# Elementwise work taken off GpSimd, and the first layer's gates run on two DFF chunks at a time

## The chip, the cores and the metric

One NeuronCore of a Trainium2 chip runs the whole kernel. The number that counts is the device time of one launch in microseconds, as a median over runs. Engines are called by the names of the profile: PE (TensorE), DVE (VectorE), ACT (ScalarE), POOL (GpSimd) and SP (SyncE, which issues most DMAs).

## The reference, cut to what matters

Windowed attention (4 batches, 8 heads, 768 positions, head size 64) gives 3072 rows of 512 features. They go through a dense layer with a gate, and then to one of eight experts each.

```python
attn = softmax(q @ k.T / 8 + alibi_bias, local window of 96 and 8 global keys) @ v
x = attn.transpose(0, 2, 1, 3).reshape(3072, 512)
h = x @ w_in                      # w_in: 512 x 2048, float64
g = h - tanh(h)
y = g @ w_out                     # w_out: 2048 x 512, float64
e = argmax(y @ w_gate)            # 8 experts
out = softmax_max * sigmoid(y @ w_output_gate)[e] * (relu(y @ w1[e]) @ w2[e])
```

## The kernel before

**Products in parts.** Each float32 operand of a large product is split into a high part (float32r) and the low rest; a product is three matmuls: high by high, low by high, high by low.

**First layer.** The 3072 tokens are taken in 12 blocks of 256, the 2048 columns of DFF in 16 chunks of 128 (`u`). `moe_h` makes one chunk's h in PSUM: 12 matmuls of 256 columns into half of a bank of the tag `h`, which has two banks. Then come three steps. `gate` makes h squared, tanh h and a polynomial (ACT three instructions, DVE three). `gate2` makes a mask and the product, and takes h - tanh h where the mask says so. `parts` splits the result into `gh` (ACT) and `gl` (POOL). `moe_y` adds the chunk to y: six matmuls of 512 columns, three for each half of the block's tokens.

**Weights of the first layer.** w_in and w_out come as float64 in 32 pieces of 128x512. `m1_split` turns the 64 bits of a number into a float32 with shifts, and then into two parts. Pieces with an even number are decoded by one ACT and three DVE instructions, DVE makes the high part and POOL the low one. Pieces with an odd number take two ACT instructions, one on POOL and two on DVE, ACT makes the high part and POOL the low one.

**Order.** `at(gt, rank, fn)` puts work on an agenda of half units: chunk `u` of block `blk` has its `moe_h` at half unit 32 blk + 2u, its `gate`, `gate2` and `parts` one, two and three half units later, and its `moe_y` four later (five in the last block). Block 0's attention begins at half unit -26. The pieces of the weights are decoded from half unit -31 to 21, so during block 0's attention and its first layer. Later blocks' attention (`plan_att`) lies among the chunks of the block before. `plan_route` sends a finished block's rows to their experts (`rt_evac`, `rt_T`, `rt_logits`, then a scatter that POOL issues). A scheduler that simulates a time line turns the agenda into the order of each engine's instructions. After the last block come eight experts, whose weights are loaded and split meanwhile (`ex_load`, `ex_split`); a first job of 256 rows (`ex_s1`, `ex_s2` of job 0) lies beside the last block's routing.

The lines that matter below: L254 to L273 decode the weights, L491 to L512 are the softmax, L580 is `moe_h`, L595 to L620 are the three steps of the gate, L637 is `moe_y`.

Of the kernel before, what the change touches and what calls it, by code (L numbers as in the profile page):

```python
# [9 lines left out]
F32 = mybir.dt.float32  # L10
# [8 lines left out]
# (h - tanh(h)) / h^3 as a cubic in u = h*h for u <= G_T2, in the form  # L19
# G_C3 * (u + G_C) * ((u + G_A)^2 + G_B); relative error below 3e-7  # L20
# [12 lines left out]
def kernel(  # L33
# [27 lines left out]
    # rows in the static part, for the experts in the order of their tokens  # L61
# [9 lines left out]
    LATE = 3                      # chunks of the last product of all, taken tile by tile  # L71
    W = DM + 2                    # a routed row: y, its scale, its token
# [106 lines left out]
    def load_next(which):  # L179
        if nxt[which] < len(pair_seq):  # L180
# [10 lines left out]
            else:  # L191
# [5 lines left out]
                # the general attention's result where that ran  # L197
# [8 lines left out]
    # weights of the first layer: four groups of four chunks of DFF  # L206
# [11 lines left out]
    def m1_load(i):  # L218
# [14 lines left out]
    def m1_split(i, gt):  # L233
        """float64 bits to float32 (its 24 leading bits), then to two parts"""
# [48 lines left out]
    # ------------------------------------------------------------ constants  # L283
    def constants_first():
# [4 lines left out]
        # value = float(low word) + 2^32 * float(high word)  # L289
# [6 lines left out]
        # the windowed path needs 1 <= n_local <= 97 and n_global <= 32  # L296
# [8 lines left out]
        # where not so, the windowed path takes each token's own value: n_global = 0, n_local = 1  # L305
# [9 lines left out]
    # minus the distance, and -BIG where not kept; a head's scores are taken over its slope  # L315
# [3 lines left out]
    # for each pair of heads, 1 / (8 slope) of the head of a row of the transposed queries  # L319
# [5 lines left out]
    def masks():  # L325
# [35 lines left out]
        # other tiles: columns 0..31 are keys 0..31, column c >= 32 has rel = p + 128 - c  # L361
        d1 = tmp("d1", "gg", 2)
# [10 lines left out]
        # a block's first tile has the same columns in another order  # L373
# [6 lines left out]
    def constants_late():  # L380
# [3 lines left out]
        # tri[k, m] = 1 where k < m  # L384
# [1003 lines left out]
```

## Time and profile before

| | before |
|---|---|
| runs | 1212.83, 1214.79, 1216.89 us (median 1214.79) |
| span of the profiled execution | 1207.3 us, from its first to its last instruction |
| PE busy | 1135.9 us (94%) |
| DVE busy | 904.5 us (75%) |
| ACT busy | 652.1 us (54%) |
| POOL busy | 321.0 us (27%) |

No time is listed for the profiled execution apart from its span. The median of the runs lies 7.5 us above that span (5.5 to 9.6 us for the three), for what a launch does before the first and after the last instruction. Busy shares are means over the span; the stages differ, so the rows below are taken by stage.

### The profile page before, as it was taken

Reading aid. Unit: us, or ns where it says so; the run is one execution under the profiler, and the core shown is the slowest. Engines: PE = TensorE matmul, PEld = TensorE weight load, DVE = VectorE, ACT = ScalarE, POOL = GpSimd, SP = SyncE. Lnnn points to the kernel's source line nnn. Section 1 sums busy time; section 2 is a strip of 40 time slices with the busy share of each in tenths; the row PEclk is TensorE's granted clock in tenths of the full one; section 3 lists DMA queues with packets and bytes.
Section 4 is the critical chain, followed back from the end, with each engine's and each line's share of the span. In section 5 each row is a group of like instructions: output and inputs, shape, how many; then the busy total and the mean of one; then the engine's idle time right before and its main releaser. Section 6 shows DMA issues by size and latency. Waiting matters only on the chain. (4 is left out here: it accounts for less than half of the span.)

```text
span 1207.3 us, 22194 instructions
## 1 busy us (share of the span) xinstructions
PE 1135.9 (94%) x7374; PEld 955.2 (79%) x7374; DVE 904.5 (75%) x2712; ACT 652.1 (54%) x1729; POOL 321.0 (27%) x377
## 2 busy tenths in 40 slices
PE   4876699999999999999999999999899999999996
PEld 3555578888888888888888888888788787888895
DVE  7999997989898889888898888899654434435410
ACT  4666576666657566657566666656443323324411
POOL 3467663423131222222222212233200101101100
PEclk9997899999999999999999999999999999999998
DMA  6643383111111111111111112012365415326200
GB/s 176 176 144 123 111 231 97 49 30 47 42 48 32 45 32 46 38 49 34 37 34 40 47 26 54 8 53 87 124 215 178 134 66 198 124 78 216 108 22 23
DMA packets 128848, 103.23 MB, mean 86 GB/s; under 512 B 101679, under 2 KB 101679, under 8 KB 128720
## 3 DMA queue, kind: packets, MB, share of 16 engines
q1 hardware_dynamic: 124592, 89.06, 25.3%
q0 software_dynamic: 4128, 12.61, 2.7%
q8 instruction: 61, 1.00, 0.3%
q14 instruction: 67, 0.55, 0.2%
HBM read 90.04 MB, written 21.88 MB: 93 GB/s over the span
## 5 line engine op out<-in xcount | busy, mean ns | idle before, releaser
L620 POOL TENSOR_TENSOR gl<-gg,gh 128x256 fp32r<-128x256 f32 x192 | 163.1, 850 | 432.0 <-ACT gh L619 367.6
L580 PE MATMUL ph<-xhi,wh 128*128 128x256 f32 x768 | 224.3, 293 | 10.1 <-DVE tt L599 10.1
L580 PE MATMUL ph<-xlo,wh 128*128 128x256 f32 x768 | 222.0, 289 | 0.1
L580 PE MATMUL ph<-xhi,wl 128*128 128x256 f32 x768 | 221.6, 289 | 0.0
L637 PE MATMUL y<-wh,gh 128*128 128x512 f32 x384 | 162.8, 424 | 7.0 <-ACT gh L619 7.0
L580 PEld LDWEIGHTS ph<-xhi,wh 128*128 128x128 f32 x768 | 148.1, 193 | 23.4 <-DVE tt L599 13.1
L580 PEld LDWEIGHTS ph<-xlo,wh 128*128 128x128 f32 x768 | 148.3, 193 | 10.6 <-issue 2.2
L637 PE MATMUL y<-wl,gh 128*128 128x512 f32 x384 | 153.5, 400 | 0.0
L580 PEld LDWEIGHTS ph<-xhi,wl 128*128 128x128 f32 x768 | 148.4, 193 | 5.6 <-issue 2.2
L637 PE MATMUL y<-wh,gl 128*128 128x512 f32 x384 | 142.2, 411 | 4.6 <-POOL gl L620 4.6
L619 ACT CAST gh<-gg 128x256 fp32r<-128x256 f32 x192 | 78.1, 407 | 122.7 <-DVE gg L613 101.2
L953 DVE SCALAR_TENSOR_TENSOR h2l<-h2p,h2h 128x448 fp32r<-128x448 f32 (+3 forms) x72 | 39.9, 557 | 102.2 <-ACT h2h L952 102.2
L875 DVE TENSOR_TENSOR el<-ex,eh 128x1024 fp32r<-128x1024 f32 x64 | 77.7, 1223 | 50.0 <-ACT eh L874 49.7
L993 POOL DMA_INDIRECT out_dram<-orow,ix x29 | 30.2, 1041 | 291.4 <-ACT orow L988 284.7
L595 ACT ACTIVATE uu<-ph 128x256 f32<-128x256 f32 x192 | 73.0, 380 | 63.7 <-PE ph L580 58.3
L598 DVE SCALAR_TENSOR_TENSOR vt<-uu,ph 128x256 f32<-128x256 f32 x192 | 79.5, 414 | 32.6 <-ACT tt L596 30.9
L952 ACT ACTIVATE h2h<-h2p 128x448 fp32r<-128x448 f32 (+3 forms) x72 | 35.3, 493 | 123.3 <-PE h2p L948 123.0
L874 ACT CAST eh<-ex 128x1024 fp32r<-128x1024 f32 x64 | 66.5, 1049 | 63.8 <-DMA ex<-in_moe_w_dram 48.8
L499 ACT ACTIVATE pr<-pr,sst 128x256 f32<-128x256 f32 (+1 forms) x192 | 92.6, 485 | 13.2 <-DVE sst L491 13.0
L613 DVE COPY_PREDICATED gg<-ss,tt 128x256 f32<-128x256 int32 x192 | 94.6, 493 | 4.9 <-POOL gg L610 1.9
L597 ACT ACTIVATE ss<-uu,ga 128x256 f32<-128x256 f32 x192 | 97.9, 511 | 0.0
L975 PE MATMUL ob<-eh,h2h 128*128 128x512 f32 x232 | 92.8, 400 | 5.3 <-ACT h2h L952 5.1
(194 smaller groups left out, 2686.6 us busy)
## 6 DMA issues: line engine op xcount, KB each, us to landing
ex<-in_moe_w_dram SPq DMA_DIRECT2D x64, 512.0 KB
vv<-vg SPq DMA_DIRECT2D x92, 96.0 KB
srt<-zrow SPq DMA_DIRECT2D x32, 257.0 KB
m<-in_moe_w_in_dram SPq DMA_DIRECT2D x16, 512.0 KB
m<-in_moe_w_out_dram SPq DMA_DIRECT2D x16, 512.0 KB
xr<-srt SPq DMA_DIRECT2D x25, 257.0 KB
qk<-in_q_dram SPq DMA_DIRECT2D x92, 64.0 KB
qk<-in_k_dram SPq DMA_DIRECT2D x92, 64.0 KB
```

Of the source, the lines that this page charges most:

```text
L499: nc.scalar.activation(pr[j][:, c0:], pr[j][:, c0:], AF.Exp, bias=st[:, j : j + 1], scale=-1.0, accum_out=st[:, 2 + j : 3 + j],)
L580: nc.tensor.matmul(ph[:, 0:TB], lw, xx[blk][:, kc, :], start=(n == 0), stop=(n == 3 * KC - 1))
L595: nc.scalar.activation(uu, hps, AF.Square)
L597: nc.scalar.activation(ss, uu, AF.Square, scale=G_S, bias=ga[:, 0:1])
L598: nc.vector.scalar_tensor_tensor(out=vv, in0=uu, scalar=G_C, in1=hps, op0=ALU.add, op1=ALU.mult)
L613: nc.vector.copy_predicated(gg, ss.bitcast(I32), tt)
L619: nc.scalar.copy(gh, gg)
L620: nc.gpsimd.tensor_tensor(out=gl, in0=gg, in1=gh.bitcast(F32), op=ALU.subtract)
L637: nc.tensor.matmul(yb[blk, j], gx[:, j * P : (j + 1) * P], wx[fg][:, sl], start=(u == 0 and n == 0), stop=(u == NF - 1 and n == 2),)
L874: nc.scalar.copy(hi, st)
L875: nc.vector.tensor_tensor(out=ld[e, t][:, sl], in0=st, in1=hi.bitcast(F32), op=ALU.subtract)
L975: nc.tensor.matmul(ob[n, j][0:m, :], gx[:, j * P : j * P + m], wx, start=(f == 0 and i == 0), stop=(f == NF2 - 1 and i == 2),)
```

## The change

In the decode, every piece now goes the way of the even ones, except that ACT makes the high part and DVE the low one. POOL has no part in it.

`moe_h` fills a whole bank with two chunks, `u` and `u + 1`, and only the second of them starts the gate. Each step of the gate then works on 512 columns. The product of `gate2` is on DVE in all blocks, the mask is a Relu on ACT in all blocks (before, in block 0 alone; DVE made it in the others), and the result stays in the tile `vt`. `parts` makes `gl` on DVE. `moe_y` stands two half units later (at 6, and at 7 in the last block), and so does the routing. The tiles change tags: `uu`, `tt` and `gl` share four of 512 columns, `ss` has one, `gh` two. POOL keeps its indirect DMAs, constants and the token numbers of the rows.

```diff
     def m1_split(i, gt):
...
-        by_pool = i % 2 == 1
         def decode():
-            if by_pool:
-                nc.gpsimd.tensor_tensor(out=tw, in0=tw, in1=st[:, :, 1], op=ALU.add)
-                nc.vector.tensor_scalar(out=w_0, in0=w_0, scalar1=29, scalar2=None, op0=ALU.logical_shift_right)
-                nc.vector.scalar_tensor_tensor(
-                    out=ti, in0=ti, scalar=3, in1=w_0, op0=ALU.logical_shift_left, op1=ALU.bitwise_or
-                )
-                return
             nc.vector.tensor_scalar(out=ti, in0=ti, scalar1=3, scalar2=None, op0=ALU.logical_shift_left)
...
         def parts():
-            if i % 2:
-                nc.scalar.copy(hi, tw)
-            else:
-                nc.vector.tensor_copy(hi, tw)
-            nc.gpsimd.tensor_tensor(out=lo, in0=tw, in1=hi.bitcast(F32), op=ALU.subtract)
+            nc.scalar.copy(hi, tw)
+            nc.vector.tensor_tensor(out=lo, in0=tw, in1=hi.bitcast(F32), op=ALU.subtract)
-        nc.scalar.activation(tw, st[:, :, 1], AF.Relu if by_pool else AF.Copy, scale=2.0**-112)
-        if by_pool:
-            nc.scalar.activation(st[:, :, 1], st[:, :, 1], AF.Relu, scale=-(2.0**-80))
+        nc.scalar.activation(tw, st[:, :, 1], AF.Copy, scale=2.0**-112)
...
     def moe_h(blk, u, gt):
-        ph = bank("h", 2, f"ph{blk}_{u}")
+        if u % 2 == 0:
+            ph_t[blk] = bank("h", 2, f"ph{blk}_{u}")
+        ph = ph_t[blk]
+        o_h = (u % 2) * TB
...
-                nc.tensor.matmul(ph[:, 0:TB], lw, xx[blk][:, kc, :], start=(n == 0), stop=(n == 3 * KC - 1))
+                nc.tensor.matmul(
+                    ph[:, o_h : o_h + TB], lw, xx[blk][:, kc, :], start=(n == 0), stop=(n == 3 * KC - 1)
+                )
+        if u % 2 == 0:
+            return
         def tmp(tag, bufs, dt=F32):
-            t = p1.tile([P, TB], dt, tag=tag, bufs=bufs, name=f"{tag}{blk}_{u}")
+            t = p1.tile([P, 2 * TB], dt, tag=tag, bufs=bufs, name=f"{tag}{blk}_{u}")
...
         def gate2():
-            gg = L["gg"] = tmp("gg", 2)
-            if blk < 1:
-                nc.scalar.activation(ss, uu, AF.Relu, bias=nt2[:, 0:1])
-            else:
-                nc.vector.tensor_scalar(out=ss, in0=uu, scalar1=G_T2, scalar2=None, op0=ALU.is_gt)
-            if blk < 2:
-                nc.gpsimd.tensor_tensor(out=gg, in0=vv, in1=uu, op=ALU.mult)
-            else:
-                nc.vector.tensor_tensor(out=gg, in0=vv, in1=uu, op=ALU.mult)
-            nc.vector.copy_predicated(gg, ss.bitcast(I32), tt)
+            nc.vector.tensor_tensor(out=vv, in0=vv, in1=uu, op=ALU.mult)
+            nc.scalar.activation(uu, uu, AF.Relu, bias=nt2[:, 0:1])
+            nc.vector.copy_predicated(vv, uu.bitcast(I32), tt)
         def parts():
-            nc.scalar.copy(gh, gg)
-            nc.gpsimd.tensor_tensor(out=gl, in0=gg, in1=gh.bitcast(F32), op=ALU.subtract)
-            g_t[blk, u] = (gh, gl)
+            gh = tmp("gh", 2, F32R)
+            nc.scalar.copy(gh, vv)
+            gl = tmp("uu", 4, F32R)
+            nc.vector.tensor_tensor(out=gl, in0=vv, in1=gh.bitcast(F32), op=ALU.subtract)
+            for i in range(2):
+                sl = slice(i * TB, (i + 1) * TB)
+                g_t[blk, u - 1 + i] = (gh[:, sl], gl[:, sl])
...
     def plan_route(blk, gt):
+        gt += 2
...
-            at(g + (5 if blk == NBLK - 1 else 4), 4, lambda blk=blk, u=u: moe_y(blk, u))
+            at(g + (7 if blk == NBLK - 1 else 6), 4, lambda blk=blk, u=u: moe_y(blk, u))
```

## Rows read from the trace of the kernel before

**Rows 1.** Stretches of the span: length, busy time of each engine, TensorE clock, DMA.

```profile
0.00:175.00 175.00, 124.98 (x695) 93.71 (x695) 164.78 (x398) 108.56 (x283) 100.08 (x110) 0.92 0.52 155
175.00:825.00 650.00, 650.00 (x4823) 555.79 (x4822) 571.75 (x1974) 408.73 (x1227) 173.92 (x224) 1.00 0.18 45
825.00:885.00 60.00, 55.18 (x354) 45.85 (x353) 43.96 (x136) 28.55 (x62) 16.95 (x17) 1.00 0.36 122
```

**Rows 2.** What PE waited for in the first 175 us: total, times, longest.

```profile
PE ph L580 <- DVE tt L599: 10.1, 8, 3.1
PE y L637 <- ACT gh L619: 6.3, 4, 1.9
```

**Rows 3.** DVE groups, first 175 us, decode: busy us, mean ns | idle before.

```profile
L256 DVE SCALAR_TENSOR_TENSOR m1t<-m1t,m 128x512 int32<-128x512 int32 x16 | 15.2, 949 | 0.0
L264 DVE SCALAR_TENSOR_TENSOR m<-m 128x512 int32<-128x512 int32 x12 | 14.3, 1194 | 0.0
...
L261 DVE SCALAR_TENSOR_TENSOR m<-m 128x512 int32<-128x512 int32 x12 | 12.7, 1054 | 0.0
L255 DVE TENSOR_SCALAR m<-m 128x512 int32<-128x512 int32 x16 | 12.6, 789 | 0.0
...
L260 DVE TENSOR_SCALAR m<-m 128x512 int32<-128x512 int32 x12 | 8.0, 665 | 0.0
L272 DVE CAST wh<-m 128x512 fp32r<-128x512 f32 x12 | 7.5, 625 | 0.0
...
L264 DVE SCALAR_TENSOR_TENSOR m1t<-m,m1t 128x512 int32<-128x512 int32 x4 | 4.6, 1146 | 0.0
...
L272 DVE CAST wh<-m1t 128x512 fp32r<-128x512 f32 x4 | 1.8, 452 | 0.0
```

**Rows 4.** DVE groups of the same stretch: softmax and gates.

```profile
L512 DVE TENSOR_SCALAR pr<-pr,sst 128x256 f32<-128x256 f32 x32 | 18.8, 629 | 0.1
...
L613 DVE COPY_PREDICATED gg<-ss,tt 128x256 f32<-128x256 int32 x17 | 13.2, 778 | 0.0
...
L600 DVE SCALAR_TENSOR_TENSOR vt<-ss,vt 128x256 f32<-128x256 f32 x18 | 9.9, 549 | 0.0
...
L598 DVE SCALAR_TENSOR_TENSOR vt<-uu,ph 128x256 f32<-128x256 f32 x18 | 7.3, 408 | 0.1
...
L506 DVE TENSOR_SCALAR sst<-sst 128x2 f32<-128x2 f32 x20 | 6.0, 307 | 0.0
```

**Rows 5.** DVE in order of time, two short stretches: start us, length us.

```profile
81.72 0.68 DVE L264 SCALAR_TENSOR_TENSOR m<-m 128x512 int32<-128x512 int32 x1
82.32 0.55 DVE L452 TENSOR_TENSOR kT<-pk,kT 128x384 fp32r<-128x384 f32 x1
82.79 0.41 DVE L600 SCALAR_TENSOR_TENSOR vt<-ss,vt 128x256 f32<-128x256 f32 x1
83.12 0.41 DVE L255 TENSOR_SCALAR m<-m 128x512 int32<-128x512 int32 x1
83.46 0.15 DVE L507 RECIPROCAL sst<-sst 128x2 f32<-128x2 f32 x1
...
505.82 0.29 DVE L608 TENSOR_SCALAR ss<-uu 128x256 f32<-128x256 f32 x1
506.02 0.42 DVE L612 TENSOR_TENSOR gg<-vt,uu 128x256 f32<-128x256 f32 x1
```

**Rows 6.** ACT groups of the first 175 us.

```profile
L276 ACT ACTIVATE m1t<-m 128x512 f32<-128x512 f32 x20 | 13.5, 674 | 5.8 <-DMA m<-in_moe_w_in_dram 4.3 <-POOL wl L273 1.5
...
L270 ACT CAST wh<-m1t 128x512 fp32r<-128x512 f32 x16 | 9.9, 618 | 8.4 <-DVE m1t L256 8.4
```

**Rows 7.** One chunk's gate in block 4 or later, first step, on ACT.

```profile
509.56 0.39 ACT L595 ACTIVATE uu<-ph 128x256 f32<-128x256 f32 x1 [1.25 <-PE ph L580]
```

**Rows 8.** The same gate, last step, on POOL.

```profile
514.07 0.74 POOL L620 TENSOR_TENSOR gl<-gg,gh 128x256 fp32r<-128x256 f32 x1 [1.34 <-ACT gh L619]
```

**Rows 9.** What PE waited for from 800 us on.

```profile
PE y L637 <- POOL gl L620: 2.3, 2, 1.7
```

More of the change, by code (lines that the diff above doesn't have):

```diff
@@ L331, in tmp @@
             return t
-        col_i = tmp("col_i", "gh", 3, I32)
+        col_i = tmp("col_i", "gh", 2, I32)
         nc.gpsimd.iota(col_i, pattern=[[1, 256]], base=0, channel_multiplier=0)
-        rel_i = tmp("rel_i", "gh", 3, I32)
+        rel_i = tmp("rel_i", "gh", 2, I32)
         nc.gpsimd.iota(rel_i, pattern=[[-1, 256]], base=P, channel_multiplier=1)
-        col = tmp("col", "uu", 2)
+        col = tmp("col", "uu", 4)
         nc.vector.tensor_copy(col, col_i)
-        rel = tmp("rel", "uu", 2)
+        rel = tmp("rel", "uu", 4)
         nc.vector.tensor_copy(rel, rel_i)
-        loc = tmp("loc", "tt", 2)
-        d0 = tmp("d0", "tt", 2)
-        kp = tmp("kp", "gg", 2)
+        loc = tmp("loc", "uu", 4)
+        d0 = tmp("d0", "uu", 4)
+        kp = tmp("kp", "ss", 1)
         r0 = rel[:, P:256]
@@ L360, in masks @@
         nc.vector.tensor_tensor(out=mask0, in0=kp[:, :P], in1=d0[:, :P], op=ALU.subtract)
-        d1 = tmp("d1", "gg", 2)
+        d1 = tmp("d1", "vt", 2)
         k1 = tmp("k1", "vt", 2)
@@ L388, in constants_late @@
         nc.gpsimd.memset(acc_oh, 0.0)
-        ci = p1.tile([P, 256], I32, tag="gl", bufs=3, name="const_i")
+        ci = p1.tile([P, 256], I32, tag="ss", bufs=1, name="const_i")
         dsc = ci[:, 0:16].rearrange("p (a b) -> p a b", a=2)
@@ L481, in biased @@
             early = blk == 0 and t == 1
-            tags = (("gh", 3), ("gl", 3)) if early else (("pr", 5), ("pr", 5))
-            pool = p1 if early else pa
             pr = L["pr"] = []
-            for j in range(2):
-                p_j = pool.tile([P, 256], F32, tag=tags[j][0], bufs=tags[j][1], name=f"pr{j}_{nm}")
-                pr.append(p_j)
+            if early:
+                both = p1.tile([P, 512], F32, tag="gh", bufs=2, name=f"pr_{nm}")
+                pr += [both[:, 0:256], both[:, 256:512]]
+            else:
+                for j in range(2):
+                    p_j = pa.tile([P, 256], F32, tag="pr", bufs=5, name=f"pr{j}_{nm}")
+                    pr.append(p_j)
             st = L["st"] = p1.tile([P, 6], F32, tag="st", bufs=3, name=f"sst{nm}")
@@ L570 @@
     yb = {}
+    ph_t = {}
     def moe_h(blk, u, gt):
         fg, fo = divmod(u, 4)
-        ph = bank("h", 2, f"ph{blk}_{u}")
+        if u % 2 == 0:
+            ph_t[blk] = bank("h", 2, f"ph{blk}_{u}")
+        ph = ph_t[blk]
+        o_h = (u % 2) * TB
         n = 0
@@ L589, in gate @@
         def gate():
-            hps = ph[:, 0:TB]
-            uu = L["uu"] = tmp("uu", 2)
-            ss = L["ss"] = tmp("ss", 2)
-            tt = L["tt"] = tmp("tt", 2)
+            uu = L["uu"] = tmp("uu", 4)
+            ss = tmp("ss", 1)
+            tt = L["tt"] = tmp("uu", 4)
             vv = L["vv"] = tmp("vt", 2)
-            nc.scalar.activation(uu, hps, AF.Square)
-            nc.scalar.activation(tt, hps, AF.Tanh)
+            nc.scalar.activation(uu, ph, AF.Square)
+            nc.scalar.activation(tt, ph, AF.Tanh)
@@ L597, in gate @@
             nc.scalar.activation(ss, uu, AF.Square, scale=G_S, bias=ga[:, 0:1])
-            nc.vector.scalar_tensor_tensor(out=vv, in0=uu, scalar=G_C, in1=hps, op0=ALU.add, op1=ALU.mult)
-            nc.vector.tensor_tensor(out=tt, in0=tt, in1=hps, op=ALU.subtract)
+            nc.vector.scalar_tensor_tensor(out=vv, in0=uu, scalar=G_C, in1=ph, op0=ALU.add, op1=ALU.mult)
+            nc.vector.tensor_tensor(out=tt, in0=tt, in1=ph, op=ALU.subtract)
             nc.vector.scalar_tensor_tensor(out=vv, in0=ss, scalar=G_S2B, in1=vv, op0=ALU.add, op1=ALU.mult)
@@ L613, in gate2 @@
[L613 to L621 removed]
+            uu, tt, vv = L["uu"], L["tt"], L["vv"]
+            nc.vector.tensor_tensor(out=vv, in0=vv, in1=uu, op=ALU.mult)
+            nc.scalar.activation(uu, uu, AF.Relu, bias=nt2[:, 0:1])
@@ L623, in moe_h @@
+            nc.vector.copy_predicated(vv, uu.bitcast(I32), tt)
+        def parts():
+            vv = L["vv"]
+            gh = tmp("gh", 2, F32R)
[5 more added lines that the diff above has]
+                g_t[blk, u - 1 + i] = (gh[:, sl], gl[:, sl])
         at(gt + 1, 0, gate)
@@ L682, in rt_logits @@
                 )
-        ps = p1.tile([P, TB], F32, tag="gg", bufs=2, name=f"lgp{blk}")
+        yl = p1.tile([P, W], F32, tag="yt", bufs=3, name=f"lgp{blk}")
+        ps = yl[:, 0:TB]
         nc.scalar.copy(ps, pp[:, 0:TB])
@@ L797, in plan_route @@
         for j in range(2):
-            g = gt + (8, 9)[j]
+            g = gt + (6, 7)[j]
             at(g, 2, lambda j=j, g=g: rt_T(blk, j, g))
-        at(gt + 14, 2, lambda: rt_logits(blk, gt + 14))
+        at(gt + 12, 2, lambda: rt_logits(blk, gt + 12))
     def counts(name):
@@ L814, in order_experts @@
         pc = counts("ord_c")
-        tmp = p1.tile([P, 256], F32, tag="uu", bufs=2, name="ord_t")
+        tmp = p1.tile([P, 256], F32, tag="uu", bufs=4, name="ord_t")
         t3 = tmp[:, 0:64].rearrange("p (a b) -> p a b", a=E)
@@ L918, in ex_T @@
                 )
-        w = 4 if N == 256 else 2
+        w = 4 if n == 0 else 2
         o = (g * nk) % w
@@ L1099, in general_attention @@
                     )
-                xo = p1.tile([P, D], F32, tag="uu", bufs=2, name=f"g_xo{t}")
+                xo = p1.tile([P, D], F32, tag="uu", bufs=4, name=f"g_xo{t}")
                 nc.scalar.copy(xo, px[:, 0:D])
@@ L1161 @@
     pools.update({
-        ("xTh", 0): (p1, "xhi", 2), ("xTl", 0): (p1, "xlo", 2), ("hh", 0): (p1, "gh", 3), ("hl", 0): (p1, "gl", 3),
+        ("xTh", 0): (p1, "xhi", 2), ("xTl", 0): (p1, "xlo", 2), ("hh", 0): (p1, "gh", 2), ("hl", 0): (p1, "uu", 4),
         ("orow", 0): (persist, "row", 3),
```

4 lines of the change are left out of this document (removed).

## The prediction

> **What bounds the kernel now.** I read the busy time by stages first. It falls into three [rows 1]. From 175 to 825 us, which is nearly all of the first layer, PE is busy for all of its 650.00 us at full clock; DVE has 571.75, ACT 408.73. Nothing that shortens an elementwise engine gives time there; a change can only lose there, by making PE wait. From 0 to 175 us, the head (block 0's attention, the decode of the weights, block 0's first layer), PE has 124.98 us and a mean clock of 0.92, so some 50 us are idle, while DVE has 164.78 of 175. At 825 to 885, the handover to the experts, PE lacks 4.8 us.
>
> Then I read what PE waits for in the head: the longest is a bank of h that DVE has not read yet (10.1 us), and another is ACT's `gh` (6.3), which follows DVE's select [rows 2]. So the head is paced by DVE.
>
> Third, I read what fills DVE there. The groups say that it hardly ever idles, but that its instructions are long [rows 3, 4]. The shift L256 takes 949 ns in the mean, L264 1194, the scaling L512 629, the select L613 778. In order of time the same forms can be seen unhindered [rows 5]: L264 0.68 us long with the next one 0.60 behind it, L255 0.41 (0.34 to the next), L600 with 256 columns 0.41 (0.33), L608 0.29 (0.20). L598, which reads one operand from PSUM, has 408 ns in the head, as it should unhindered; the stretched forms have all operands in SBUF. POOL is busy for 100.08 us of the head [rows 1], with two-operand work in SBUF. I read the stretch as DVE standing while POOL holds the way to SBUF. If so, much of DVE's busy time in the head is waiting, and it goes with POOL's work.
>
> **The change, part by part, in the head.** I count from one start to the next, which is 0.08 us less than the length (0.68 against 0.60, 0.41 against 0.33 [rows 5]).
>
> Decode. Before: 8.0 + 12.7 + 14.3 + 7.5 for twelve even pieces, 12.6 + 15.2 for sixteen odd ones, and four rows for the last four even pieces, of which the first and last stand in the group and which I take together at 12 us: 82 us for 96 instructions [rows 3], less 96 x 0.08, is 74.5 us (unhindered it would be 16 x 1.88 + 16 x 0.94 = 45). After: each of 32 pieces has L260 (two-port form, 0.34) and three of 512 columns with two operands (0.60 each), so 2.14 us, 68.5 in all. The instructions taken from POOL are paid out of the waiting that goes: a gain of 6 us.
>
> Gates. Before, for 18 chunks: 13.2 + 9.9 + 7.3, and L599, which reads the same bank, taken like L598: 37.7 us, less 71 x 0.08, is 32.0 [rows 4]. After, for nine pairs: six instructions of 512 columns at 0.60, 32.4 us. The two that DVE takes over (the product and `gl`) are paid by the wider form, since 256 columns more cost 0.27 and not 0.33, and by the lost waiting. No gain, no loss.
>
> Attention isn't edited, but it is hindered too. L512: 18.8 less 32 x 0.08 is 16.2; unhindered it is the form of L608, 0.20 x 32 = 6.4. Gain 9.8. L506 has 307 ns for two columns against 0.15 us of L507 beside it: 20 x 0.15 = 3 us [rows 4, 5].
>
> DVE's sum: 6 - 0.4 + 9.8 + 3 = 18.4 us less of 165.
>
> ACT. Each piece now has one scaling (674) and one cast (618 [rows 6]): 41.4 us; before, 16 pieces had two scalings and a cast and 16 one scaling, 42 us. The gates get fewer, wider instructions. With 108.56 of 175 us [rows 1] ACT isn't the bound. But the casts of the even pieces (L272, two-port, 0.34 on DVE) and the mask now pass from DVE to ACT and back, where ACT's queue of attention and gate work stands behind a cast that waits for DVE.
>
> How much of the 18.4 us arrives depends on how far DVE stays fed. The bounds: it stays as full as now, and all arrives; or it idles 12%, as it does beside a saturated PE (571.75 of 650 [rows 1]), and the remaining 146 us of work take 146 / 0.88 = 166, as now, so nothing arrives. The nearer row is the head's own, with its queue always full, but the new hops cost something. I take 5% of 146, 7 us: 11 us gained.
>
> On that hop a rule speaks against the change. The Trainium skill, ScalarE: Activation LUTs, Rules for kernel authors, says that relu, max and plain arithmetic belong on VectorE. By it the mask would stay on DVE, which is 9 x 0.34 = 3 us more of DVE's sum in the head, 15.4 in place of 18.4, and one hop less in the chain. The rows of this case speak for ACT as long as DVE sets the pace, since ACT has 56 us less work in the head [rows 1].
>
> **The steady stage.** The bank of h is now refilled two chunks later than it is read, so the wait of 10.1 us [rows 2] should shrink; the tiles turn over in time too (by the agenda a pair's `uu`, `tt` and `gl` are free three half units or more before their slot comes round). What gets longer is the chain from h to `gl`. Before, it ran from 509.56 to 514.81, 5.2 us with a blocked stretch in it [rows 7, 8]. After, by 512 columns: three on ACT, then DVE, the mask on ACT, the select, `gh` on ACT, `gl` on DVE. Nine steps at 0.6 to 0.7 us, of which two overlap, make 5 to 6 us, plus queues. For the second chunk of a pair `moe_y` stands a whole chunk later than before, which covers it (650 us for some 11 blocks of 16 chunks [rows 1], 3.7 us a chunk). For the first chunk the distance from the pair's end to its `moe_y` is as before, four half units. I cost it at nothing: PE's queue has two chunks of `moe_h` and attention ahead, and DVE, with 6 x 0.60 a pair in place of twelve of 256 columns, has more room.
>
> PE's own work doesn't change: the same matmuls. SP's loads keep their order; a staging slot of an odd piece comes free when DVE has decoded it, where POOL had to take part.
>
> **The handover.** The last `moe_y` and the routing stand two half units later, so about 3 us of job 0's work is used up earlier, which can leave PE idle by as much before job 1's rows arrive. Against that, the 2.3 us of waits for `gl` [rows 9] and POOL's late work there go. Net nothing, within 3 us.
>
> **Sum.** 1207.3 - 11 = 1196.3 us of span; the median of the runs lies 7.5 above the span, so 1204 us.
>
> **The rivals.**
> *The whole stretch goes.* If DVE keeps full and the wider bank also takes away most of PE's waits, the head shortens by 18.4 us or more, up to 28 if the 10.1 us on the bank come on top: 1187 to 1196. For it: the waits all lead to DVE. Against: they overlap with what I already counted.
>
> *The head is paced by something else.* With POOL's way clear, the casts and masks through ACT, or loads, keep the pace: 0 to 4 us, and with the handover's 3 us lost 1209 to 1218. For it: DMA is at 0.52 of its share in the head [rows 1], and 32 pieces cross engines three times. Against: DVE idles nowhere there now.
>
> *The pair's chain is late in the steady stage (the other side).* PE would stand before the first chunk's `moe_y` in each pair. The stage has about 87 pairs (192 chunks less 18, halved [rows 4]). It eats the head's gain from 11 / 87 = 0.13 us a pair; at 0.35 us it costs 30, net 19: 1234. For it: the chain was 5.2 us and may now be 6 with queues, and the distance in the agenda is the same. Against: PE has no wait at all there now, with DVE at 88%, and DVE gets lighter.
>
> **How the numbers follow.** The forecast has 0.50 (1196 to 1209 by itself), the larger gain 0.12, the neutral head 0.20, the late chain 0.18. A measurement of this kernel can tell 0.3%, 3.6 us: under 1211.1 is faster, over 1218.4 slower. Faster has the first two and a fifth of the third, 0.66; the same 0.16; slower 0.18. The range from 1187 to 1222 leaves out the far part of the late chain and a little below.
>
> **What would show it.** Right: POOL almost empty; L256 gone, L261 and L264 near 0.68 us; L512 near 0.29 in the head; PE gap-free from about 164 us on, not 175; no wait for `gh` or `gl` in the steady stage. Wrong: DVE with idle time in the head and ACT named as the one it waits for; or PE under 650 of 650 in the stage behind it, with `gh` or `gl` as releaser; or more than 8 us lost between the last block and job 1.

## The result and the profile after

Five runs of the changed kernel took 1218.34 to 1224.73 us, median 1222.22, against 1214.79 before: a ratio of 1.0065, with a 95% interval of 1.0042 to 1.0088. It is slower by more than the 0.3% that can be told from no change, where faster was forecast, and 0.22 us above the range. The profiled execution has a span of 1220.1 us (before 1207.3).

The same stretches as in [rows 1], after (busy us of PE, PEld, DVE, ACT and POOL, then PE's clock, DMA share, GB/s):

```profile
0.00:175.00 175.00, 132.21 (x794) 105.46 (x795) 152.85 (x434) 111.05 (x259) 4.80 (x30) 0.82 0.64 181
175.00:825.00 650.00, 646.62 (x4752) 550.28 (x4751) 509.10 (x1491) 417.16 (x958) 29.95 (x41) 1.00 0.16 39
825.00:885.00 60.00, 51.81 (x306) 44.33 (x305) 35.98 (x79) 27.24 (x46) 3.84 (x5) 0.91 0.23 80
```

The head did what it was forecast to do: 794 matmuls in 175 us in place of 695, DVE 12 us less busy. The loss is behind it. DVE's groups of the head, to be held against [rows 3, 4] (busy us, mean ns, idle before):

```profile
L255 DVE SCALAR_TENSOR_TENSOR m1t<-m,m1t 128x512 int32<-128x512 int32 x20 | 13.7, 685 | 0.0
L261 DVE TENSOR_TENSOR wl<-m1t,wh 128x512 fp32r<-128x512 f32 x20 | 13.7, 684 | 0.0
L252 DVE SCALAR_TENSOR_TENSOR m1t<-m,m1t 128x512 int32<-128x512 int32 x20 | 13.6, 685 | 0.0
L499 DVE TENSOR_SCALAR pr<-pr,sst 128x256 f32<-128x256 f32 x36 | 10.9, 347 | 0.0
L251 DVE TENSOR_SCALAR m1t<-m1t 128x512 int32<-128x512 int32 x20 | 8.4, 422 | 1.7 <-ACT m1t L264 1.7
...
L493 DVE TENSOR_SCALAR sst<-sst 128x2 f32<-128x2 f32 x22 | 3.5, 164 | 0.1
```

The forms that took 949 to 1194 ns take 685; the softmax's scaling (L512 before, L499 now) went from 629 to 347, the two-column one (L506, L493) from 307 to 164.

To see where time is lost behind the head I take the moment at which ACT starts to move a block's finished y out of PSUM (`yrow`): of block 0, of block 10 and of block 11, the last. The kernel before:

```profile
176.44 0.59 ACT L652 ACTIVATE yrow<-y 128x512 f32<-128x512 f32 x1
...
805.94 0.60 ACT L652 ACTIVATE yrow<-y 128x512 f32<-128x512 f32 x1 [0.48 <-PE y L637]
...
855.67 0.60 ACT L652 ACTIVATE yrow<-y 128x512 f32<-128x512 f32 x1 [3.25 <-PE y L637]
```

And after:

```profile
166.37 0.60 ACT L644 ACTIVATE yrow<-y 128x512 f32<-128x512 f32 x1 [1.05 <-PE y L629]
...
800.50 0.60 ACT L644 ACTIVATE yrow<-y 128x512 f32<-128x512 f32 x1 [2.95 <-PE y L629]
...
864.08 0.60 ACT L644 ACTIVATE yrow<-y 128x512 f32<-128x512 f32 x1 [0.83 <-PE y L629]
```

Block 0 is done 10.1 us earlier. The ten blocks behind it take 634.13 us and not 629.50: 4.6 lost. The last takes 63.6 and not 49.7: 13.9 lost. From there to job 1's first output it is 60.2 us against 58.5, and from that to the last output 2.9 us more are lost. -10.1 + 4.6 + 13.9 + 1.7 + 2.9 = 13.0, and the spans differ by 12.8. (The medians differ by 7.4, since one execution was profiled of each, and that of before was a quick one: wherever a run's span is listed, the time lies 1.7 to 2.2 us above the span, so a span of 1207.3 us stands for about 1209 us, an estimate. The 7.5 us that were put down to the launch are mostly this. The forecast, 11 us under the median, doesn't hang on it.) So the last block holds the loss. What PE waited for from 795 us on, after (total, times, longest):

```profile
PE y L629 <- ACT gh L608: 10.2, 5, 4.5
PE xTp L910 <- DMA xr<-srt: 5.4, 2, 5.2
```

and before, beside [rows 9]:

```profile
PE xTp L916 <- DMA xr<-srt: 1.6, 2, 1.3
PE y L637 <- ACT gh L619: 0.7, 3, 0.3
```

The last block as a stretch, in the columns of above, after and before:

```profile
800.50:864.08 63.58, 52.51 (x310) 44.54 (x309) 44.83 (x86) 34.51 (x57) 3.81 (x4) 0.92 0.28 92
805.94:855.67 49.73, 45.37 (x289) 37.98 (x288) 46.40 (x125) 29.85 (x72) 20.40 (x19) 1.00 0.30 100
```

PE idles for 11.1 us of it in place of 4.4, which is 6.7 of the 13.9 us. About 4.5 us are work of job 0 that has moved ahead of the last y: 24 matmuls of its first product (`h2p`), 4 of its second (`ob`) and 6 more that transpose its rows (`xTp`), where before only 2 transposes stood; the 4.5 are an estimate at 0.12, 0.23 and 0.11 us each. Against that 14 fewer h matmuls fall into the stretch, 1.7 us. The 4.4 us that are left stand beside a clock of 0.92 against 1.00.

What makes `gh` late is in ACT's queue. In this stretch of the last block the cast of `gh` (L608) stands behind two casts of expert 0's weights (L868), which wait for their loads; DVE's select, its operand, had started at 825.77 and lasted 0.76 us:

```profile
825.01 0.72 ACT L602 ACTIVATE uu<-uu,nt 128x512 f32<-128x512 f32 x1 [2.28 <-DVE vt L600]
826.79 1.04 ACT L868 CAST eh<-ex 128x1024 fp32r<-128x1024 f32 x1 [1.06 <-DMA ex<-in_moe_w_dram]
829.72 1.04 ACT L868 CAST eh<-ex 128x1024 fp32r<-128x1024 f32 x1 [1.88 <-DMA ex<-in_moe_w_dram]
830.67 0.61 ACT L608 CAST gh<-vt 128x512 fp32r<-128x512 f32 x1
831.19 0.59 ACT L591 ACTIVATE uu<-ph 128x512 f32<-128x512 f32 x1
```

Later in the block no cast is left, and the bare cycle can be read, from one mask (L602) to the next:

```profile
846.71 0.72 ACT L602 ACTIVATE uu<-uu,nt 128x512 f32<-128x512 f32 x1 [2.59 <-DVE vt L600]
848.26 0.62 ACT L608 CAST gh<-vt 128x512 fp32r<-128x512 f32 x1 [0.83 <-DVE vt L603]
848.78 0.60 ACT L591 ACTIVATE uu<-ph 128x512 f32<-128x512 f32 x1
849.27 0.59 ACT L592 ACTIVATE uu<-ph 128x512 f32<-128x512 f32 x1
849.75 0.72 ACT L593 ACTIVATE ss<-uu,ga 128x512 f32<-128x512 f32 x1
852.60 0.72 ACT L602 ACTIVATE uu<-uu,nt 128x512 f32<-128x512 f32 x1 [2.13 <-DVE vt L600]
```

It is 5.89 us long, and in it stands one pair at a time: the next pair's first square (L591) comes behind this pair's `gh`, so ACT waits 2.13 us for DVE's product and 0.83 for its select with nothing else to do. PE needs about 5.6 us for a pair by its own rows, 24 matmuls of h at one per 0.12 us and 12 of y at one per 0.23:

```profile
808.42 0.28 PE L573 MATMUL ph<-xlo,wh 128*128 128x256 f32 x1
808.54 0.28 PE L573 MATMUL ph<-xhi,wl 128*128 128x256 f32 x1
...
812.77 0.39 PE L629 MATMUL y<-wl,gh 128*128 128x512 f32 x1
813.00 0.40 PE L629 MATMUL y<-wh,gh 128*128 128x512 f32 x1
```

In the steady blocks attention stands between the products and a pair has 7.9 us (63.4 / 8). In the last block it has 5.6, so the cycle is the longer of the two, and each cast (1.04 us and its wait) that ACT takes in between comes on top: `gh` follows `gh` by 7.8, 11.1, 11.2, 6.4, 5.9 and 5.9 us from 811.77 on.

### The profile page after: what moved, and what is told of

The parts are those of the page before. It is cut to its first block, busy times and chain, and to the rows that moved or that the text cites. A ratio compares the mean times of both kernels' runs of the same rounds, so it can differ in the third digit from the quotient of the medians.

```text
span 1220.1 us, 20873 instructions
## 1 busy us (share of the span) xinstructions
PE 1143.2 (94%) x7374; PEld 965.1 (79%) x7374; DVE 824.4 (68%) x2216; ACT 663.4 (54%) x1425; POOL 69.0 (6%) x105
## 5 line engine op out<-in xcount | busy, mean ns | idle before, releaser
L629 PE MATMUL y<-wl,gh 128*128 128x512 f32 x384 | 156.7, 408 | 0.0
L629 PE MATMUL y<-wh,uu 128*128 128x512 f32 x384 | 147.6, 421 | 2.3 <-DVE uu L610 2.3
L602 ACT ACTIVATE uu<-uu,nt 128x512 f32<-128x512 f32 x96 | 69.4, 723 | 100.6 <-DVE vt L600 82.5
L629 PEld LDWEIGHTS y<-wh,gh 128*128 128x128 f32 x384 | 74.7, 195 | 33.1 <-ACT gh L608 16.8
L942 PE MATMUL h2p<-xTh,eh 128*128 128x448 f32 (+3 forms) x288 | 98.6, 346 | 0.0
L942 PE MATMUL h2p<-xTl,eh 128*128 128x448 f32 (+3 forms) x288 | 98.7, 343 | 0.0
L942 PE MATMUL h2p<-xTh,el 128*128 128x448 f32 (+3 forms) x288 | 98.0, 341 | 0.0
L603 DVE COPY_PREDICATED vt<-uu,uu 128x512 f32<-128x512 int32 x96 | 72.3, 753 | 35.8 <-ACT uu L602 35.0
L868 ACT CAST eh<-ex 128x1024 fp32r<-128x1024 f32 x64 | 66.2, 1048 | 49.4 <-DMA ex<-in_moe_w_dram 32.7
L969 PE MATMUL ob<-el,h2h 128*128 128x512 f32 x232 | 91.3, 394 | 0.0
```

Of the source, the lines that this page charges most:

```text
L602: nc.scalar.activation(uu, uu, AF.Relu, bias=nt2[:, 0:1])
L603: nc.vector.copy_predicated(vv, uu.bitcast(I32), tt)
L629: nc.tensor.matmul(yb[blk, j], gx[:, j * P : (j + 1) * P], wx[fg][:, sl], start=(u == 0 and n == 0), stop=(u == NF - 1 and n == 2),)
L868: nc.scalar.copy(hi, st)
L942: nc.tensor.matmul(ph[:, 0:N], lw, xx, start=(i == 0), stop=(i == 3 * KC - 1))
L969: nc.tensor.matmul(ob[n, j][0:m, :], gx[:, j * P : j * P + m], wx, start=(f == 0 and i == 0), stop=(f == NF2 - 1 and i == 2),)
```

## The experiments

All were timed beside the kernel before on the same chip. The head's code is the same in many of them, and block 0 still ended anywhere from 162.7 to 167.7 us; so I compare the last block's length, from evacuation to evacuation.

| run | us | ratio to before, 95% | block 0 done | last block |
|---|---|---|---|---|
| the change | 1222.22 | 1.0065 (1.0042 to 1.0088) | 166.4 | 63.6 |
| e1_split_late | 1218.58 | 1.0052 (1.0037 to 1.0067) | 167.7 | 65.0 |
| e2_decode_only | 1197.19 | 0.9869 (0.9852 to 0.9887) | 158.3 | 49.6 |
| e3_gates_only | 1240.42 | 1.0219 (1.0199 to 1.0238) | 184.7 | 62.5 |
| e4_narrow | 1214.81 | 1.0027 (1.0008 to 1.0046) | 160.5 | 56.6 |
| e5_early_y | 1219.66 | 1.0057 (1.0037 to 1.0077) | 163.7 | 64.9 |
| e6_no_load_wait | 1224.53 | 1.0095 (1.0064 to 1.0127) | 164.5 | 67.5 |
| e7_gl_last | 1207.74 | 0.9963 (0.9942 to 0.9984) | 159.0 | 56.3 |
| e8_pool_last | 1225.10 | 1.0107 (1.0074 to 1.0140) | 163.7 | 65.7 |
| e9_more_lag | 1219.99 | 1.0062 (1.0039 to 1.0085) | 163.2 | 64.6 |
| e10_mask_dve | 1218.48 | 1.0044 (1.0021 to 1.0067) | 167.4 | 62.0 |
| e11_lag_mask | 1214.74 | 1.0016 (0.9997 to 1.0036) | 169.8 | 61.6 |
| e12_last_old | 1226.09 | 1.0124 (1.0084 to 1.0164) | 163.1 | 73.4 |
| e13_parts_late | 1220.46 | 1.0057 (1.0032 to 1.0082) | 163.4 | 63.8 |
| e14_no_cast | 1216.94 | 1.0042 (1.0025 to 1.0058) | 164.3 | 58.7 |
| e15_parts_mask | 1217.44 | 1.0041 (1.0019 to 1.0062) | 167.6 | 62.4 |
| e16_all_three | 1211.32 | 0.9982 (0.9958 to 1.0006) | 171.1 | 55.8 |
| e17_pool_cast | 1227.31 | 1.0130 (1.0098 to 1.0163) | 162.7 | 66.0 |
| e18_pool_cast_parts_mask | 1224.62 | 1.0081 (1.0047 to 1.0116) | 173.0 | 67.6 |

In all twenty traces job 1's first output comes 57 to 62 us after the last block's evacuation. So that evacuation sets the end, and the wait for job 1's rows (`xr`) is its consequence: the work of job 0 that PE does before it is missing after it.

### Which half of the change

e1: the changed kernel with expert 0's casts three half units later.

```diff
-        at(G + 12 + 2 * i, 0, lambda i=i: ex_split(0, i))
+        at(G + 15 + 2 * i, 0, lambda i=i: ex_split(0, i))
```

> The changed kernel, with each piece of expert 0's weights split three half units later in the last block (at 15 + 2i in place of 12 + 2i), nothing else. Theory A (in the last block ACT's queue holds casts of expert 0's weights that wait for their load, and the gate's gh stands behind them): PE's waits for gh from 800 to 865 us fall from 10.2 us to under 4, the last block from 63.6 to 55 us or less, the time to 1211 to 1215. Rival B (the pair's chain of nine steps is itself too long once no attention lies between the chunks): waits and time stay, 1220 to 1224.

e2: the kernel before with the new decode alone, that is the diff's hunk of `m1_split` and nothing else of it. e3: the changed kernel with `m1_split` as it was before.

> The kernel before, with only the decode of the first layer's weights changed (no POOL in it); gates single and with POOL, agenda as before. Theory A (the head gains because POOL's hold on SBUF goes; two thirds of POOL's head work is decode): block 0's rows are evacuated 6 to 10 us earlier than at 176.4, the last block is as before, time 1205 to 1209. Rival C (the head's gain comes from the wide bank of h and the pairs): 1213 to 1217, and block 0 ends at 174 or later.

> The changed kernel with the decode of before put back (POOL adds and subtracts in it); paired gates and their agenda stay. Theory A: the last block loses as in the changed kernel (waits for gh about 10 us from 800 us on) and the head gains only 2 to 6 us, time 1224 to 1232. Rival C: 1220 to 1224.

e4: e2, and nothing elementwise on POOL, but gates of single chunks, on the agenda of before.

```diff
-            if blk < 1:
-                nc.scalar.activation(ss, uu, AF.Relu, bias=nt2[:, 0:1])
-            else:
-                nc.vector.tensor_scalar(out=ss, in0=uu, scalar1=G_T2, scalar2=None, op0=ALU.is_gt)
-            if blk < 2:
-                nc.gpsimd.tensor_tensor(out=gg, in0=vv, in1=uu, op=ALU.mult)
-            else:
-                nc.vector.tensor_tensor(out=gg, in0=vv, in1=uu, op=ALU.mult)
+            nc.vector.tensor_tensor(out=gg, in0=vv, in1=uu, op=ALU.mult)
+            nc.scalar.activation(ss, uu, AF.Relu, bias=nt2[:, 0:1])
...
-            nc.gpsimd.tensor_tensor(out=gl, in0=gg, in1=gh.bitcast(F32), op=ALU.subtract)
+            nc.vector.tensor_tensor(out=gl, in0=gg, in1=gh.bitcast(F32), op=ALU.subtract)
```

> No elementwise work on POOL, but gates of single chunks, 256 columns, in the agenda and tiles of before (mask on ACT, product and gl on DVE, decode as changed). Theory A: the head gains 8 to 13 us; in the last block gh still stands behind casts of expert weights now and then, because POOL frees the staging rows as early as in the changed kernel; waits for gh 4 to 10 us from 800 us on, time 1206 to 1216. Rival B (pair chain): waits for gh under 3 us there, blocks 1 to 10 at 62.95 us each and not 63.41, time 1201 to 1206.

The two halves pull apart, and further than was expected of either: 8 us less time than the lower end of its range for e2, 8 us more than the upper end for e3. The decode alone ends block 0 18.2 us earlier and gives 1.3%; the gates alone end it 8.3 us later, make the last block 12.8 us longer and cost 2.2%. e4 lies between: 7 us of the last block go with POOL's gate work, the rest with the pairs. (Its head is 2.2 us longer than that of e2, which is less than equal heads differ by.) Waits of PE from 795 us on in e2:

```profile
PE y L622 <- POOL gl L605: 2.3, 2, 1.7
PE y L622 <- ACT gh L604: 0.4, 2, 0.2
```

The casts wait for their loads there too, 8.9 us in all in the last block, against 7.3 in the changed kernel's. But ACT holds two chunks in flight; here the square at 825.91 (L580) stands ahead of the `gh` at 826.51, and a wait of 1.80 us for a load doesn't reach PE:

```profile
824.95 1.05 ACT L859 CAST eh<-ex 128x1024 fp32r<-128x1024 f32 x1 [1.26 <-DMA ex<-in_moe_w_dram]
825.91 0.37 ACT L580 ACTIVATE uu<-ph 128x256 f32<-128x256 f32 x1
826.51 0.41 ACT L604 CAST gh<-gg 128x256 fp32r<-128x256 f32 x1 [0.23 <-DVE gg L598]
...
831.47 1.06 ACT L859 CAST eh<-ex 128x1024 fp32r<-128x1024 f32 x1 [1.80 <-DMA ex<-in_moe_w_dram]
832.43 0.40 ACT L604 CAST gh<-gg 128x256 fp32r<-128x256 f32 x1
```

e1 changed nothing that can be told: the later casts still wait (3.51 us the longest) and still stand ahead of `gh`, and PE waits 11.9 us for it.

### Loads, distance, GpSimd

e6 casts a tile that is on the chip, a weight of the first layer, so that expert 0's product is left out (first hunk); e5 puts the last block's second product earlier (second hunk) and its routing two half units earlier; e7 is e2 with `gl` on DVE in the last block (third hunk); e8 is the change with `gl` on POOL there, by the same line with the engines exchanged.

```diff
         hi = hd[e, t][:, sl]
+        if e == 0:
+            st = wih[0][:, 0:1024].bitcast(F32)
         nc.scalar.copy(hi, st)
...
-            at(g + (7 if blk == NBLK - 1 else 6), 4, lambda blk=blk, u=u: moe_y(blk, u))
+            at(g + (6 if blk < NBLK - 1 or u % 2 == 0 else 4), 4, lambda blk=blk, u=u: moe_y(blk, u))
...
-            nc.gpsimd.tensor_tensor(out=gl, in0=gg, in1=gh.bitcast(F32), op=ALU.subtract)
+            eng = nc.vector if blk == NBLK - 1 else nc.gpsimd
+            eng.tensor_tensor(out=gl, in0=gg, in1=gh.bitcast(F32), op=ALU.subtract)
```

> The changed kernel, but the casts and remainders of expert 0's weights read a weight tile that is already on the chip in place of the loaded rows (the loads are still issued; expert 0's product is left out in this sense). So no cast on ScalarE waits for a load. Theory L (a cast that waits for its load stands ahead of the gate's gh in ScalarE's queue): the last block falls from 63.6 us to about 52 to 56, the waits of PE for gh in it from 10 to under 3 us, the clock stays at 1.00 there, and the time goes from 1222 to 1206 to 1213. Theory C (the pair's longer chain by itself is late once no attention fills PE): waits for gh of 8 us or more stay, time 1218 to 1223.

> The changed kernel, but in the last block the second product stands at +6 half units for the first chunk of a pair and +4 for the second, in place of +7 for both, and the routing of the last block two half units earlier. Theory that the two half units' later second product costs the handover: the rows of job 1 are waited for 2 to 4 us less and the time is 1216 to 1219. Theory L: the casts still stand ahead of gh, and there is now less distance to hide it, so PE's waits for gh grow by what the handover gains: 1219 to 1225. Theory C: still worse, 1224 to 1230.

> The kernel before with the new decode (1197.2 us), and one more edit: gl is made on VectorE in the last block alone, so that GpSimd's queue holds nothing but the scatters and constants there. Theory S (a free GpSimd lets block 10's scatter and with it the loads of expert 0's weights start early and all at once, and their casts then stop ScalarE): the last block goes from 49.6 to 55 us or more and the time to 1204 to 1212. If what matters is the load on VectorE and ScalarE over all blocks, or the pair's chain: 1196 to 1200.

> The changed kernel with gl back on GpSimd in the last block alone (512 columns). Theory S: block 10's scatter stands behind gl on GpSimd's queue again, the loads come one by one, the last block falls from 63.6 us by 6 us or more, time 1208 to 1216. Theory C: GpSimd's 512-column gl lengthens the chain by about 0.6 us a pair, the last block is the same or longer, time 1221 to 1227.

e6 is no clean test: PE's waits for `gh` fell to 6.3 us, but the casts now waited 6.3 us for the second product, whose weights hold their tiles' room, and the last block got longer. e5 moved the handover by under 1 us and `gh` is waited for longer (11.8), on the side of a late `gh`. e7 shows that taking `gl` off POOL in the last block alone costs 6.7 us there even with single chunks. Its time is the one that theory S gave, but not for theory S's reason: block 10's scatter is issued 37.3 us after that block's evacuation against 37.8 in e2, and the casts of expert 0 start, counted from there, within 1.1 us of their times in e2. What differs is the order in the queues. Here too a cast that waits for its load stands ahead of a `gh`, and PE waits 2.99 us for it:

```profile
836.83 1.05 ACT L860 CAST eh<-ex 128x1024 fp32r<-128x1024 f32 x1 [2.64 <-DMA ex<-in_moe_w_dram]
...
838.46 0.39 ACT L604 CAST gh<-gg 128x256 fp32r<-128x256 f32 x1
```

In all PE idles 5.8 us in that block and 2.8 in e2's, and 24 `h2p`, 1 `ob` and 6 more `xTp` stand ahead of the last y, some 3.8 us by the same estimate as above: together about the 6.7. e4 has the same two parts (one wait of 5.2 us for `gh`, 24 `h2p` and 2 `ob`). And e8 shows that putting `gl` back among the pairs returns nothing, so theory S falls for the pairs as well.

### Distance and hops

e9: the second product of the last block at +9 half units (first hunk). e10: the mask on DVE in all blocks (second hunk). e11: both. e12: gates of single chunks in the last block of the changed kernel, on halves of the pair's tiles, mask on DVE, `gl` on POOL.

```diff
-            at(g + (7 if blk == NBLK - 1 else 6), 4, lambda blk=blk, u=u: moe_y(blk, u))
+            at(g + (6 if blk < NBLK - 1 else 9 if u < NF - 2 else 7), 4, lambda blk=blk, u=u: moe_y(blk, u))
...
-            nc.scalar.activation(uu, uu, AF.Relu, bias=nt2[:, 0:1])
+            nc.vector.tensor_scalar(out=uu, in0=uu, scalar1=G_T2, scalar2=None, op0=ALU.is_gt)
```

> The changed kernel, but in the last block the second product of all chunks but the last two stands at +9 half units in place of +7. Theory C (in the last block no attention stands between the products, so a pair's chain from h to gl has only four chunks of products, 5.6 us, to hide in, and takes longer than that): with 8.4 us to hide in, PE's waits for gh in the last block fall from 10.2 us to under 5, the last block from 63.6 to 54 to 58, time 1212 to 1217. If a wait that no distance hides sets the pace (casts behind loads, one chain after the other): last block over 61, time 1219 to 1223.

> The changed kernel, but the select's mask is made by VectorE (a compare in place) and not by ScalarE's Relu in place, in all blocks. In the changed kernel's last block ScalarE stands 9.4 us in its queue because that Relu overwrites a tile that VectorE's product still reads. Theory C with the hops as the cause: two hops fewer in each of 8 pairs, about 1 us a pair, and ScalarE's queue free: last block 56 to 60, time 1213 to 1218; in the head VectorE has 3 us more. If the hop is not what makes the chain long: 1222 to 1226.

> Both edits of the two runs before. Theory C: nothing of the chain is left to see, last block 50 to 54, time 1208 to 1213. If load waits or the handover set the pace: over 1217.

> The changed kernel, but the last block has the gates as they were: by single chunks of 256 columns, mask on VectorE, gl on GpSimd, second product at +5 half units, routing two half units earlier. The head and the steady blocks stay as changed. Theory that what was lost lies in the gates of the last block: last block 50 to 53 us as before, and time 1203 to 1209. If the loss sits in what the steady blocks leave for it, or in the handover: last block over 58, time over 1214.

e9 is the telling miss of theory C: more distance leaves 12.9 us of waits for `gh`. A chain that is late hides behind more distance; a cycle that is longer than PE's does not. e10 and e11 missed their ranges too. e10 shortened the cycle, gained 1.6 us there and 0.6 us in each block before, and ended with `gh` every 5.6 to 6.0 us; the casts' waits for loads grew to 16.6 us in ACT's idle time. e12 shows only that halves of shared tiles are worse: with one tile `ss` ACT waits 5.8 us for DVE before it can write the next half.

### The cycle itself

e13 puts the next pair's squares ahead of this pair's `gh` in ACT's queue (first hunk; the routing goes two half units later). e14 takes expert 0's casts out, and its product with them: it takes weights of the first layer (second hunk). e15 is e13 with e10's mask; e16 has all three, so it leaves out what e14 does. e17 is the change with the casts and remainders on POOL (third hunk), e18 is e17 with e13 and e10.

```diff
-        at(gt + 3, 0, parts)
+        at(gt + (3 if blk < NBLK - 1 else 6), 0, parts)
...
-            at(g + (7 if blk == NBLK - 1 else 6), 4, lambda blk=blk, u=u: moe_y(blk, u))
+            at(g + (6 if blk < NBLK - 1 else 10 if u < NF - 2 else 9), 4, lambda blk=blk, u=u: moe_y(blk, u))
...
+        if e == 0:
+            staged.pop(("e", e, i))
+            hd[e, t], ld[e, t] = wih[t], wil[t]
+            return
...
+        if e == 0:
+            nc.gpsimd.tensor_copy(hi, st)
+            nc.gpsimd.tensor_tensor(out=ld[e, t][:, sl], in0=st, in1=hi.bitcast(F32), op=ALU.subtract)
+            return
```

> The changed kernel, but in the last block gh and gl of a pair are issued three half units later, so that ScalarE's queue holds the next pair's squares and tanh ahead of this pair's gh; the second product stands at +10 (last two chunks +9), the routing two half units later. Theory Q (the pairs' chains run one after the other because in ScalarE's queue gh stands ahead of the next pair's first square: 5.9 us a pair by itself against 5.6 us of PE, and all that is put between, casts with their waits above all, adds to it): with two pairs in flight gh comes every 4.5 to 5.6 us where nothing is put between, PE's waits for gh fall from 10.2 us to under 6, the last block from 63.6 to 54 to 59 us, time 1213 to 1218. If the loads behind the casts set the pace: last block over 62, 1220 to 1224.

> The changed kernel without the casts and remainders of expert 0's weights (its product takes weights of the first layer in their place; the loads are still issued and nothing reads them). Theory Q: the pairs' chains are still one after the other, but with nothing but routing between them: 6 to 7 us a pair, waits of PE for gh of 2 to 6 us in all, last block 50 to 55 us, time 1206 to 1212. If the casts only fill time in which ScalarE would wait anyway: last block over 60, time over 1217.

> The edit of the late parts and the mask on VectorE together. Theory Q: last block 52 to 57, time 1208 to 1214, at or under the kernel before. If the loads behind the casts set the pace: 1215 to 1219, as with the mask alone.

> The changed kernel with three edits at once: gh and gl of a pair behind the next pair's first squares in the last block, the mask on VectorE, and no casts of expert 0's weights (its product takes weights of the first layer in their place). Theory Q (the last block is paced by the pairs' chains one after the other, with the casts and the mask's hop in the same cycle): nothing is left in the cycle but routing, the last block falls from 63.6 us to 50 to 55, and the end follows the last evacuation by about 60 us of first outputs as in all runs: time 1202 to 1210. If the place of job 0's work, or what the steady blocks leave over, sets the last block: over 58 us, time over 1214.

> The changed kernel, but the casts and remainders of expert 0's weights are made by GpSimd, which is busy for 3.8 of 65 us there. Theory Q: as without the casts, last block 57 to 61 us, time 1214 to 1219; but they now stand in the queue of the scatters, and a block's rows may come later: then over 1221.

> The three edits of the first run of this group with nothing left out: the casts on GpSimd, the late parts, the mask on VectorE. Theory Q: last block 52 to 58 us, time 1206 to 1213. If loads or scatters set the pace: over 1217.

PE's waits for `gh` and for rows from 795 to 870 us in e14:

```profile
PE xTp L914 <- DMA xr<-srt: 3.9, 1, 3.9
PE y L629 <- ACT gh L608: 3.8, 3, 1.4
```

And the same view of e16:

```profile
PE y L629 <- ACT gh L608: 1.8, 1, 1.8
PE xTp L914 <- DMA xr<-srt: 0.8, 1, 0.8
```

Without the casts 4.9 of the 13.9 us come back, with all three edits 7.8, and the wait for `gh` is all but gone: 10.2, 5.9 (e13), 3.8 (e14), 1.8. That bears theory Q out as to the wait, and not as to the time: e13, e14 and e15 all missed the ranges that it gave, and e13 and e15 came out in those of its rival, loads that set the pace. The traces show what the shorter wait was lost to. In e13 PE idles 8.0 us in the last block in place of 11.1, but 41 `h2p` and 12 `ob` of job 0 stand ahead of the last y in place of 24 and 4, which is 3.9 us more by the estimate of above: the evacuation is as late. (ACT also waits 6.2 us there for y matmuls that still read its tiles.) In e16 these are 43 and 12, where e2 has none of either. There PE idles for only 2.8 us, less than the 4.4 of before, and the block is still 6 us longer. Since the end follows the evacuation, job 0's work isn't free there, and e16 missed its 50 to 55 us by 0.8 and its time by 1.3. No run held job 0's products back behind the last y, so what their place costs by itself is read from the traces and not tested.

e17 and e18, which leave nothing out, fail for the reason that the prediction began with, as far as the trace tells (that the scatters stand in the same queue was not tried apart). The remainder takes POOL 2.7 us a piece, and DVE's instructions with both data operands in SBUF stretch beside it while those that read PSUM don't. One L600 (at 845.45) that began beside a remainder lasted 2.73 us, L595 (at 843.48), with a remainder beside it all the time, 0.68; L610, which reads SBUF alone as well, has a mean of 703 ns, and none of its five began beside a remainder. DVE's groups from 815 to 855 us in e17; L600 and L596 took 689 and 684 ns in the changed kernel:

```profile
L600 DVE TENSOR_TENSOR vt<-vt,uu 128x512 f32<-128x512 f32 x5 | 8.3, 1660 | 0.2
L596 DVE SCALAR_TENSOR_TENSOR vt<-ss,vt 128x512 f32<-128x512 f32 x5 | 7.9, 1582 | 0.0
...
L594 DVE SCALAR_TENSOR_TENSOR vt<-uu,ph 128x512 f32<-128x512 f32 x5 | 3.4, 686 | 1.1 <-ACT uu L592 1.1
L595 DVE TENSOR_TENSOR uu<-uu,ph 128x512 f32<-128x512 f32 x5 | 3.4, 680 | 0.0
```

The Trainium skill (GPSIMD Engine Reference, 1. Specifications) says that GpSimd's way to SBUF is shared with VectorE and that they contend where a DVE instruction has two SBUF inputs; the trace agrees, by the 1660 against 686 ns above.

## Why the prediction was wrong

**The head: right, with one term wrong.** A piece costs DVE 422 + 685 + 685 + 684 ns less 4 x 0.08 us, 2.16 us (forecast 2.14). The stretch went with POOL's work, also in L499 and L493, which nobody edited. Block 0 came 10.1 us earlier (forecast 11). But "No gain, no loss" for the gates was wrong: e3 shows +8.3 us in the head, and the decode alone -18.2. So the 11 came out by luck in part, as the sum of a larger gain and a loss that wasn't forecast. The second product two half units later, about 3.7 us of the loss by the prediction's chunk time, is one part of it. Another can be read in e3's trace: in the first 175 us PE waits 20.5 us for the softmax's scaled rows (`pr`, DVE), against 8.5 before. Why they come later, and the split, stay open. The sum had no term for the clock, which was 0.82 in the head in place of 0.92 in these two executions.

**The steady stage: no wait, and yet 4.6 us.** "I cost it at nothing" held as to waits: 0.5 us from 175 to 795, at full clock. Still the ten blocks take 634.1 us in place of 629.5. Part of that is the head's gain paid back: block 1 alone takes 1.6 us longer (62.8 against 61.2), and in e2, which has the gates of before, 3.6 us (64.8) while the nine blocks behind it agree with before within 0.1 us. In the slower head PE had done more of block 1's work before block 0 was done (449 matmuls fall between the two evacuations in the kernel before, 479 in e2). The other 3.0 us are lost in blocks 2 to 10 with the pairs; with the mask on DVE (e10) they are not, these blocks take 566.8 us against 571.3 and 568.3 before. Why was not found.

**The failed step** is the pair's chain: "For the first chunk the distance from the pair's end to its `moe_y` is as before, four half units. I cost it at nothing: PE's queue has two chunks of `moe_h` and attention ahead". In the last block no attention is left to stand ahead. The chain was sized a little short: from the square at 848.78 to the end of that pair's `gl` at 855.50 it is 6.7 us with nothing in between (forecast 5 to 6, plus queues). But what went wrong is that it was held against a distance; what counts is that the pairs follow one another without overlap, one per 5.9 us at best, against the 5.6 us that PE needs for a pair. The rival *The pair's chain is late in the steady stage* had the mechanism and put it in the wrong place: nothing in some 87 pairs, and 10.2 us of waits for `gh` in the last block's eight, because the casts of expert 0 stand in the same queue. Shown: the gates of the pairs cost it (e2, e3), casts and lost overlap make up PE's wait for `gh` (e13, e14, e16). Read from the traces and not tested: job 0's products, which the scheduler put ahead of the last y, for about 4.5 of the 13.9 us. Of the 13.9 us, e4 and e7 put about 7 on `gl` leaving POOL, even with single chunks; there too it is a cast ahead of `gh`, and job 0's products. Why the scheduler's order changes so much with that one move stays open.

**The handover: right as put.** "Net nothing, within 3 us" holds once it is counted from the last evacuation (60.2 us against 58.5). But the "3 us of job 0's work" that would be "used up earlier" are some 4.5, they lie in the last block, and the wait for job 1's rows grew from 1.6 to 5.4 us.

**The mask on DVE.** The rule of the Trainium skill (ScalarE: Activation LUTs, Rules for kernel authors) was weighed as 3 us of the head. The trace of e10 leans its way: last block 1.6 us and ten blocks 5.9 us shorter; but the ratio, 1.0044, lies within the change's interval.

The best version is e2, the decode alone: 1197.19 us, 1.3% under the kernel before and 2% under the change.

## What to carry to other kernels

Cost a longer chain at every place where it runs, above all where the work that hides it ends: a chain whose turns don't overlap is held against the cycle of the engine it feeds, not against the distance in the schedule, and each foreign instruction in its queues adds its wait. Look too at what a scheduler moves ahead of the work that sets the end. Try the halves of a change apart before joining them: here one half was worth 1.3% and the other cost 2.2%. The Trainium skill (Perfetto Trace Analysis, Optimizing Scalar/DVE Operations) advises smaller instructions where ACT and DVE aren't full and yet leave gaps on another engine; the trace agrees: single chunks gave 56.6 us in the last block (e4), pairs 63.6, with DVE busy for 44.8 of these and ACT for 34.5.

## What the runs showed of the hardware

A gap can cost more than its length here. The granted clock by stretches of 10 us, after:

```profile
820.00:830.00 10.00, 6.14 (x36) 1.00 0.52 159
830.00:840.00 10.00, 8.66 (x39) 0.66 0.60 210
840.00:850.00 10.00, 7.78 (x40) 0.83 0.17 52
...
890.00:900.00 10.00, 8.72 (x42) 0.57 1.03 354
```

and before, with PE busy for 7.52 of 10 us:

```profile
840.00:850.00 10.00, 7.52 (x42) 1.00 0.37 125
```

After the waits of 4.51 us (at 831) and 5.2 us (at 891) PE runs for a while at 1.2 of 2.4 GHz: the y matmuls behind the first follow each other by 0.43 us (831.93, 832.36) and not by 0.23. The short gaps of before, 1.7 us the longest, brought no such drop. But in e2 one of 1.72 us did, with y matmuls 0.43 us apart behind it (836.82, 837.25):

```profile
830.00:840.00 10.00, 8.07 (x34) 0.83 0.51 179
```

So the length of a gap alone doesn't tell whether the clock falls. Of the 13.9 us a part is lost clock.
